# Tap matrices in the array's diagonal quadrants, and another order of the first half blocks, in a convolution followed by a two-layer MLP

## The chip, the cores and the metric

The kernel runs on one core of one Trainium2 chip. The time is device microseconds from launch to end, the median of several runs. A profile covers one execution; its span (first to last instruction) is some 1.7 us less than the time of the same run. Line numbers in profiles are those of the kernel profiled, so the same statement is L341 in one kernel and L356 in another; the tile names say which it is: ph is the first matmul of the MLP, po the second, acc the convolution on TensorE, ptr the transposes, yt the convolution's result, g the activated hidden layer.

## The reference

```python
# x: [8, 4096, 192] f32, weight: [8 heads, 7 taps], w_in: [192, 2048], w_out: [2048, 192]
w = softmax(weight, axis=-1)                      # 7 taps per head, 24 channels share a head
x_pad = concatenate([zeros(B, 6, D), x], axis=1)
out = einsum('hk,bskhg->bshg', w, windows(x_pad))   # causal convolution along the sequence
h = out.reshape(B * S, D) @ w_in
return maximum(0.01 * h, h) @ w_out
```

## The kernel before

Two batch rows are worked on together: partitions 0 to 63 hold 64 channels of one, 64 to 127 the same channels of the other. The sequence is cut into blocks of 512; the first five blocks are handled as ten groups of 256 ("half groups", numbered from 0). Halves 0 to 3 are loaded by plain transfers, cast and transposed on TensorE; later blocks come through transposing transfers. For groups 0 and 1 TensorE does two of the three channel chunks of the convolution, by multiplying with diagonal tap matrices; VectorE does everything else of it, one group ahead of TensorE.

```python
    diag = [const_pool.tile([128, 2, K, 128], BF16, name=f"diag{c}") for c in range(NPEC)]
    def diag_high(c):                     # high bf16 part of the 7 taps: VectorE, 896 elements
        nc.vector.tensor_mul(diag[c][:, 0], ident[:, None, :].to_broadcast([128, K, 128]),
                             wkh[:, c, :, None].to_broadcast([128, K, 128]))
    def diag_low(c, ks):                  # low part: ScalarE, 128 elements a tap
        for k in ks:
            nc.scalar.activation(out=diag[c][:, 1, k, :], in_=ident, func=Copy, scale=wkl[:, c, k : k + 1])
    ...
    load_first(2)
    for job in conv_jobs(groups[0], range(NPEC, NCH)): job()        # third chunk, VectorE
    for c in range(NPEC):                                           # two chunks, TensorE
        pe_jobs, evac_y = pe_conv_jobs(groups[0], c)                # 14 matmuls 128x128 by 128x256
        for job in pe_jobs: job()
        evac_y(act_scale)
        warm(3)
    ...
    for i, grp in enumerate(groups):
        ...
        for j in range(steps):
            for u in range(2 * j, 2 * j + 2):
                mm1(grp, u)               # 12 ph matmuls, then one activation on ScalarE
                ...                       # i == 0: transposes of half 1, TensorE's convolution of group 1
            for _ in range(quota):
                mm2_slot(slot); slot += 1     # po matmuls, two row halves
            for job in ahead[per * j : per * (j + 1)]: job()    # VectorE: convolution of group i+1
            if i == 0 and j == 2:
                for evac_y in evacs: evac_y(nc.vector.tensor_scalar_mul)
                for e in range(2): cast_first(2, e, nc.vector.tensor_copy)
            if i == 1 and j == 2:
                for e in range(2): cast_first(3, e, nc.vector.tensor_copy)
            if i < 2 and j == 3:
                transpose_first(i + 2)
                evac_first(i + 2, nc.vector.tensor_copy, nc.vector.tensor_copy)
```

Of the kernel before, what the change touches and what calls it, by code (L numbers as in the profile page):

```python
# [10 lines left out]
BF16 = mybir.dt.bfloat16  # L11
# [3 lines left out]
def kernel(  # L15
# [8 lines left out]
    nc = tc.nc  # L24

    B, S, D = x.shape
    H, K = weight.shape
# [3 lines left out]
    BASE = HALO - (K - 1)  # L31
# [3 lines left out]
    CH = 64  # L35
    NCH = D // CH
    ST = 512
# [9 lines left out]
    NPEC = 2  # L47

    const_pool = ctx.enter_context(tc.tile_pool(name="const", bufs=1))
# [14 lines left out]
    groups = [(b, h * HT, HT) for b in range(NHALF) for h in range(2)]  # L64
# [3 lines left out]
    x_nat, x_bf, xt = {}, {}, {}  # L68
# [35 lines left out]



    def load_first(q):
        t = stage_pool.tile([128, 2, HS, D], FP32, name="x_nat")
        for e in range(2):
            nc.sync.dma_start(  # L110
                out=t[:, e, :, :],
                in_=x[e, q * HT : (q + 1) * HT, :].rearrange("(c p) d -> p c d", p=128),
            )
        x_nat[q] = t

    def cast_first(q, e, copy):
        if q % 2 == 0 and e == 0:
            x_bf[q // 2] = xb_pool.tile([128, NCH, SUB, 2, CH], BF16, name="x_bf")
        h = q % 2
        copy(  # L120
            out=x_bf[q // 2][:, :, h * HS : (h + 1) * HS, e, :],
            in_=x_nat[q][:, e, :, :].rearrange("p s (c k) -> p c s k", c=NCH),
        )
# [3 lines left out]
    def transpose_first(q):  # L127
        ts = [
            psum_o.tile([128, HS, NCH, CH], BF16, name=f"ptr{i}", tag="po") for i in range(2)
        ]  # L130
        for s in range(HS):
            for c in range(NCH):
                for i in range(2):
                    ps = slice(i * CH, (i + 1) * CH)
                    nc.tensor.transpose(  # L135
                        out=ts[i][:, s, c, :],
                        in_=x_bf[q // 2][ps, c, (q % 2) * HS + s, :, :].rearrange(
                            "p e k -> p (e k)"
                        ),
                        identity=ident[ps, ps],  # L140
                    )
        ptr[q] = ts

    def evac_first(q, *copies):
        dst = xt[0][:, :, HALO + q * HT : HALO + (q + 1) * HT].rearrange(
            "p c (s i k) -> p i s c k", s=HS, i=2
        )
        for i, t in enumerate(ptr.pop(q)):
            copies[i](out=dst[:, i], in_=t)  # L149
# [4 lines left out]
    def conv_jobs(grp, chunks=range(NCH)):  # L154
        blk, t0, T = grp
        rp, st = divmod(blk, NB)
        if blk not in yt:
            yt[blk] = yt_pool.tile([128, NCH, ST], BF16, name="yt")
        y = yt[blk]
        jobs = []  # L160
        for c in chunks:
            for k in range(K):
                a = BASE + k + st * ST + t0
                src = xt[rp][:, c, a : a + T]
                dst = y[:, c, t0 : t0 + T]
                if k == 0:
                    jobs.append(
                        lambda s=src, d=dst, c=c: nc.vector.tensor_scalar_mul(  # L168
                            d, s, wk[:, c, 0:1]
                        )  # L170
                    )
                else:
                    jobs.append(
                        lambda s=src, d=dst, c=c, k=k: nc.vector.scalar_tensor_tensor(  # L174
                            out=d, in0=s, scalar=wk[:, c, k : k + 1], in1=d,
                            op0=mybir.AluOpType.mult, op1=mybir.AluOpType.add,
                        )
                    )
        return jobs

    def pe_conv_jobs(grp, c):


        blk, t0, T = grp
        acc = psum_o.tile([128, ST], FP32, name="acc", tag="po")
        jobs = []
        for p in range(2):
            for k in range(K):
                jobs.append(
                    lambda k=k, p=p: nc.tensor.matmul(  # L190
                        out=acc[:, :T], lhsT=diag[c][:, p, k, :],
                        rhs=xt[0][:, c, BASE + k + blk * ST + t0 : BASE + k + blk * ST + t0 + T],
                        start=(k == 0 and p == 0), stop=(k == K - 1 and p == 1),
                    )
                )
        return jobs, lambda scale: scale(yt[blk][:, c, t0 : t0 + T], acc[:, :T], rsum[:, c, :])  # L196


# [8 lines left out]
    nc.vector.memset(junk, 0.0)  # L207
    ident = const_pool.tile([128, 128], BF16)
    make_identity(nc, ident)

    sel = const_pool.tile([H, NCH, 2, CH], FP32, name="sel")
    nc.gpsimd.memset(sel, 1.0)  # L212
    for sign, off in ((1, 0), (-1, GRP - 1)):
        nc.gpsimd.affine_select(  # L214
            out=sel, in_=sel, compare_op=mybir.AluOpType.is_ge, fill=0.0,
# [4 lines left out]
    w_in = const_pool.tile([128, NCH, F], BF16)  # L220
    for q in range(WQ):
        for e in range(2):
            fs = slice(q * F // WQ, (q + 1) * F // WQ)
            nc.gpsimd.dma_start(  # L224
                out=w_in[e * CH : (e + 1) * CH, :, fs],
                in_=moe_w_in[:, fs].rearrange("(c p) f -> p c f", p=CH),
# [7 lines left out]
    def warm(n):  # L234
# [9 lines left out]
        out=nmax, in_=w9[:, 0:K], axis=mybir.AxisListType.X,  # L244
# [3 lines left out]
        out=w9[:, 0:K], in_=w9[:, 0:K], func=mybir.ActivationFunctionType.Exp,  # L248
# [4 lines left out]
    for c in range(NCH):  # L253
        nc.tensor.matmul(
            out=wps[:, 0, c * (K + 1) : (c + 1) * (K + 1)],
# [12 lines left out]
    nc.vector.tensor_sub(wkl, wraw[:, :, 0:K], wkh)  # L268


    diag = [const_pool.tile([128, 2, K, 128], BF16, name=f"diag{c}") for c in range(NPEC)]

    def diag_high(c):
        nc.vector.tensor_mul(  # L274
            diag[c][:, 0],
            ident[:, None, :].to_broadcast([128, K, 128]),
            wkh[:, c, :, None].to_broadcast([128, K, 128]),
        )

    def diag_low(c, ks):  # L280
        for k in ks:
            nc.scalar.activation(  # L282
                out=diag[c][:, 1, k, :], in_=ident,
                func=mybir.ActivationFunctionType.Copy, scale=wkl[:, c, k : k + 1],
            )

    transpose_first(0)
    warm(3)
    diag_high(0)
    diag_low(0, range(2))  # L290
    evac_first(0, nc.vector.tensor_copy, nc.scalar.copy)
    diag_low(0, range(2, K))
    diag_high(1)
    diag_low(1, range(K))
    rsum = const_pool.tile([128, NCH, 1], FP32)
# [7 lines left out]
            out=out, in_=in_, func=mybir.ActivationFunctionType.Copy, scale=scale  # L303
        )

    load_first(2)
    for job in conv_jobs(groups[0], range(NPEC, NCH)):
        job()
    for c in range(NPEC):
# [99 lines left out]
    for i, grp in enumerate(groups):  # L409
        blk, t0, T = grp  # L410
        steps = T // 64
        if t0 == 0:
            g[blk] = g_pool.tile([128, NFC, 2, ST], BF16, name="g", tag="g")
        quota = (avail - slot) // steps

        if i == 0:
            ahead, pe_ahead = [], []
        else:
            ahead = conv_jobs(groups[i + 1]) if i + 1 < len(groups) else []
        per = -(-len(ahead) // (steps - 1)) if T == ST else -(-len(ahead) // steps)  # L420
        for j in range(steps):
            for u in range(2 * j, 2 * j + 2):
                mm1(grp, u)
                if i == 0 and u == 1:
                    transpose_first(1)
                    evac_first(1, nc.vector.tensor_copy, nc.vector.tensor_copy)
                    ahead = conv_jobs(groups[1], range(NPEC, NCH))
                    evacs = []
                    for c in range(NPEC):
                        pe_jobs, evac_y = pe_conv_jobs(groups[1], c)  # L430
                        pe_ahead += pe_jobs
                        evacs.append(evac_y)
                    per = len(ahead)
                if i == 0 and u in (3, 5):
                    for job in pe_ahead[: 2 * K]:
                        job()
                    pe_ahead = pe_ahead[2 * K :]
            for _ in range(quota):
                mm2_slot(slot)
                slot += 1  # L440
            for job in ahead[per * j : per * (j + 1)]:
                job()
            if i == 0 and j == 2:
                for evac_y in evacs:
                    evac_y(nc.vector.tensor_scalar_mul)
                for e in range(2):
                    cast_first(2, e, nc.vector.tensor_copy)
            if i == 1 and j == 2:
                for e in range(2):
                    cast_first(3, e, nc.vector.tensor_copy)  # L450
            if i < 2 and j == 3:

                transpose_first(i + 2)
                evac_first(i + 2, nc.vector.tensor_copy, nc.vector.tensor_copy)

            last_half = t0 + T == ST
            if j == steps // 4 and last_half:
                load_x(blk + 3)
            if j == steps // 2 and last_half and blk > 0:
                transpose_x(blk + 2)  # L460
        avail += 2 * T // 128 * NFC
# [37 lines left out]
```

## Time and profile before

| | kernel before |
|---|---|
| time, first three runs | 699.71 us (699.24 to 699.77) |
| span of the profiled run | 697.3 us |
| TensorE busy | 689.5 us, 99% |
| VectorE, ScalarE busy | 541.0 us, 512.2 us |
| first ph matmul, first po matmul | 10.88 us, 23.55 us |
| start of group 2 on TensorE | 33.34 us |

In a timeline row the columns are start, length (both us), engine, line, operation, tiles, shapes, count, and in brackets the idle time before it with what ended it. A matmul row's length includes the last matmul's way through the array, so rows overlap by a little. A waits row gives who waited for whom, total us, times, and the longest.

### The profile page before, as it was taken

Reading aid. Unit: us, or ns where it says so; the run is one execution under the profiler, and the core shown is the slowest. Engines: PE = TensorE matmul, PEld = TensorE weight load, DVE = VectorE, ACT = ScalarE, POOL = GpSimd, SP = SyncE. Lnnn points to the kernel's source line nnn. Section 1 sums busy time; section 2 is a strip of 40 time slices with the busy share of each in tenths; the row PEclk is TensorE's granted clock in tenths of the full one; section 3 lists DMA queues with packets and bytes.
Section 4 is the critical chain, followed back from the end, with each engine's and each line's share of the span. In section 5 each row is a group of like instructions: output and inputs, shape, how many; then the busy total and the mean of one; then the engine's idle time right before and its main releaser. Section 6 shows DMA issues by size and latency. Waiting matters only on the chain.

```text
span 697.3 us, 25946 instructions
## 1 busy us (share of the span) xinstructions
PE 689.5 (99%) x11730; PEld 611.6 (88%) x11730; DVE 541.0 (78%) x995; ACT 512.2 (73%) x574; POOL 142.0 (20%) x198
## 2 busy tenths in 40 slices
PE   8999999999999999999999999999999999999997
PEld 6899998678888888888888888888888888888887
DVE  6799999967777787777787777787777787777712
ACT  6778887977777777777777777777777777777770
POOL 6342221420222211222220222220222211000000
PEclk9999999999999999999999999999999999999999
DMA  9986654855556545557543556534555545112112
GB/s 174 134 89 75 83 79 74 90 72 80 74 66 92 82 66 86 67 74 91 80 75 70 78 73 87 86 68 72 78 75 84 86 67 77 54 51 59 47 36 69
DMA packets 184846, 54.37 MB, mean 78 GB/s; under 512 B 148384, under 2 KB 184736, under 8 KB 184736
## 3 DMA queue, kind: packets, MB, share of 16 engines
q0 software_dynamic: 98768, 14.17, 29.4%
q1 hardware_dynamic: 85968, 38.56, 22.6%
q8 instruction: 91, 1.49, 0.9%
q14 instruction: 19, 0.16, 0.1%
HBM read 29.88 MB, written 25.17 MB: 79 GB/s over the span
## 4 chain that ended last, share of the span: by engine, by line
PE 92%; DVE 4%; DMA 3%; ACT 0%; POOL 0%; issue 0%; POOLq 0%; ACTq 0%
PE po L361 47%; PE ph L341 45%; DVE yt L174 3%; DMA w_out<-in_moe_w_out_dram 2%; DMA w_in<-in_moe_w_in_dram 1%; ACT g L348 0%; DVE yt L168 0%; POOL sel L214 0%; DVE xt L149 0%; POOL sel L212 0%; PE ptr L135 0%; DVE o_sb L400 0%; POOL ident masks.py:199 0%; ACT o_sb L400 0%; POOL ident masks.py:197 0%
## 5 line engine op out<-in xcount | busy, mean ns | idle before, releaser
L348 ACT ACTIVATE g<-ph 128x1024 bf16<-128x1024 f32 x512 | 496.2, 1021 | 165.6 <-PE ph L341 165.6
L174 DVE SCALAR_TENSOR_TENSOR yt<-xt,wk,yt 128x512 bf16<-128x512 bf16 (+1 forms) x642 | 439.7, 685 | 17.4
L361 PE MATMUL po<-w_out,g 64*128 64x192 bf16 (+1 forms) x8048 | 397.8, 243 | 0.1
L361 PEld LDWEIGHTS <-g 64*128 64x128 bf16 (+1 forms) x8048 | 372.1, 94 | 28.8 <-issue 0.4
L341 PE MATMUL ph<-yt,w_in 64*128 64x512 bf16 (+1 forms) x3552 | 391.9, 347 | 2.5 <-DVE yt L174 1.4
L341 PEld LDWEIGHTS <-w_in 64*128 64x128 bf16 x3552 | 249.1, 94 | 48.0 <-issue 5.4
L79 POOL DMA_DIRECT2D x_bf<-in_x_dram x180 | 133.6, 772 | 433.0 <-DMA xt<-x_bf 424.9
L400 DVE COPY o_sb<-po 128x192 f32<-128x192 f32 x216 | 77.3, 358 | 127.2 <-PE po L361 124.8
L168 DVE TENSOR_SCALAR yt<-xt,wk 128x512 bf16<-128x512 bf16 (+1 forms) x107 | 36.4, 340 | 0.2
L400 ACT COPY o_sb<-po 128x192 f32<-128x192 f32 x40 | 13.1, 327 | 0.0
L190 PE MATMUL acc<-xt,diag 128*128 128x256 bf16 x56 | 7.4, 288 | 0.0
L190 PEld LDWEIGHTS <-diag 128*128 128x128 bf16 x56 | 5.6, 103 | 1.6 <-issue 0.4
L236 PE MATMUL warm<-zero 128*128 128x256 bf16 x20 | 4.5, 372 | 1.1 <-DVE junk L207 1.1
L224 POOL DMA_DIRECT2D w_in<-in_moe_w_in_dram x8 | 5.1, 643 | 0.0
L282 ACT ACTIVATE diag<-ident,wkl 128x128 bf16<-128x128 bf16 x14 | 4.3, 391 | 0.1
L236 PEld LDWEIGHTS <-zero 128*128 128x128 bf16 x20 | 2.2, 122 | 1.8 <-DVE junk L207 1.1
L120 DVE CAST x_bf<-x_nat 128x384 bf16<-128x384 f32 x7 | 2.7, 416 | 1.4 <-DMA x_nat<-in_x_dram 1.4
L149 DVE COPY xt<-ptr 128x384 bf16<-128x384 bf16 x7 | 2.2, 354 | 1.8 <-PE ptr L135 1.8
L196 DVE TENSOR_SCALAR yt<-acc,rsum 128x256 bf16<-128x256 f32 x2 | 1.0, 483 | 2.6 <-PE acc L190 2.6
L274 DVE TENSOR_TENSOR diag<-ident,wkh 128x896 bf16<-128x896 bf16 x2 | 2.2, 1082 | 0.0
L135 PEld LDWEIGHTS <-x_bf 64*128 64x128 bf16 x48 | 1.2, 101 | 0.9 <-issue 0.8
L135 PE MATMUL ptr<-ident,x_bf 64*128 64x64 bf16 x48 | 1.7, 202 | 0.2 <-ACT o_sb L400 0.2
(27 smaller groups left out, 11.8 us busy)
## 6 DMA issues: line engine op xcount, KB each, us to landing
out_dram<-o_sb SPq DMA_DIRECT2D x128, 192.0 KB, 2.1
x_bf<-in_x_dram POOLq DMA_DIRECT2D x180, 64.0 KB, 3.5
x_nat<-in_x_dram SPq DMA_DIRECT2D x8, 192.0 KB, 5.9
w_in<-in_moe_w_in_dram POOLq DMA_DIRECT2D x8, 192.0 KB, 9.2
xt<-x_bf SPq DMA_TRANSPOSE x90, 2.4
w_out<-in_moe_w_out_dram POOLq DMA_DIRECT2D x1, 768.0 KB, 14.2
w<-in_weight_dram SPq DMA_DIRECT2D x1, 0.2 KB
```

Of the source, the lines that this page charges most:

```text
L79: nc.gpsimd.dma_start(out=t[:, c, :, e, :], in_=src[2 * rp + e, :, :, c * CH : (c + 1) * CH],)
L135: nc.tensor.transpose(out=ts[i][:, s, c, :], in_=x_bf[q // 2][ps, c, (q % 2) * HS + s, :, :].rearrange("p e k -> p (e k)"), identity=ident ...
L168: lambda s=src, d=dst, c=c: nc.vector.tensor_scalar_mul(d, s, wk[:, c, 0:1])
L174: lambda s=src, d=dst, c=c, k=k: nc.vector.scalar_tensor_tensor(out=d, in0=s, scalar=wk[:, c, k : k + 1], in1=d, op0=mybir.AluOpType.mult, ...
L190: lambda k=k, p=p: nc.tensor.matmul(out=acc[:, :T], lhsT=diag[c][:, p, k, :], rhs=xt[0][:, c, BASE + k + blk * ST + t0 : BASE + k + blk * ...
L224: nc.gpsimd.dma_start(out=w_in[e * CH : (e + 1) * CH, :, fs], in_=moe_w_in[:, fs].rearrange("(c p) f -> p c f", p=CH),)
L236: nc.tensor.matmul(out=wa[:, 0, 0:HT], lhsT=zero[:, 0:128], rhs=zero, start=True, stop=True)
L282: nc.scalar.activation(out=diag[c][:, 1, k, :], in_=ident, func=mybir.ActivationFunctionType.Copy, scale=wkl[:, c, k : k + 1],)
L341: nc.tensor.matmul(out=ph[:, e, i * T : (i + 1) * T], lhsT=w_in[ps, c, f * 128 : (f + 1) * 128], rhs=y[ps, c, t0 : t0 + T], start=(c == 0) ...
L348: act = nc.scalar.activation(out=g[blk][:, nf * u : nf * (u + 1), :, t0 : t0 + T], in_=ph.rearrange("p e (i t) -> p i e t", i=nf), func=my ...
L361: ins = nc.tensor.matmul(out=po[m], lhsT=g[b][ps, fc, e, s * 128 : (s + 1) * 128], rhs=w_out[ps, fc, :], start=(rt != 1 and fc == 0), stop ...
L400: copy(out=o_sb[:, n % 2, :], in_=po.pop(n))
```

## The change

Its intent is to shorten the start and to give VectorE less to do there. Each tap matrix is block diagonal with two equal 64 by 64 blocks, so it is stored folded to 64 columns and used in two diagonal quadrants of the array. The load of half 2 waits for a late instruction of ScalarE, to leave the transfers to w_in. The casts of halves 2 and 3 go from VectorE to ScalarE, the transposes are done earlier, and VectorE starts group 2's convolution before it scales the second chunk of group 1. The diff is abridged, with some lines joined.

```diff
-                        out=acc[:, :T], lhsT=diag[c][:, p, k, :], rhs=xt[0][:, c, ...],
+                for e in range(2):
+                    ps = slice(e * CH, (e + 1) * CH)
+                            out=acc[ps, :T], lhsT=diag[c][ps, p, k, :], rhs=xt[0][ps, c, a : a + T],
...
+    nc.vector.tensor_add(ident2, ident[:, 0:CH], ident[:, CH:128])
-    diag = [const_pool.tile([128, 2, K, 128], BF16, name=f"diag{c}") for c in range(NPEC)]
+    diag = [const_pool.tile([128, 2, K, CH], BF16, name=f"diag{c}") for c in range(NPEC)]
...
-    load_first(2)
+    load_first(2, low)          # the first of its two transfers waits for diag_low(0)
...
+                if i == 0 and u == 2:
+                    for e in range(2): cast_first(2, e, nc.scalar.copy)
+                if i == 0 and u == 4:
+                    transpose_first(2); evacs[0](act_scale)
+                if i == 1 and u in (0, 2): cast_first(3, u // 2, nc.scalar.copy)
...
+            if i == 0 and j == 3:
+                evac_first(2, nc.vector.tensor_copy, nc.vector.tensor_copy)
+                early = conv_jobs(groups[2])
+                for job in early[:4]: job()
+                evacs[1](nc.vector.tensor_scalar_mul)
-            if i == 0 and j == 2: ...   # scalings and casts on VectorE, as shown above
-            if i == 1 and j == 2: ...
-            if i < 2 and j == 3: ...
+            if i == 1 and j == 1: transpose_first(3)
+            if i == 1 and j == 3: evac_first(3, nc.vector.tensor_copy, nc.vector.tensor_copy)
```

More of the change, by code (lines that the diff above doesn't have):

```diff
@@ L103, in new_xt, with load_first @@
         nc.vector.memset(xt[rp][:, :, 0:HALO], 0.0)
-    def load_first(q):
+    def load_first(q, after=None):
         t = stage_pool.tile([128, 2, HS, D], FP32, name="x_nat")
         for e in range(2):
-            nc.sync.dma_start(
+            ins = nc.sync.dma_start(
                 out=t[:, e, :, :],
@@ L113, in load_first @@
             )
+            if after is not None and e == 0:
+                tc.add_manual_dep(
+                    ins.ins, after.ins.name,
+                    mybir.DependencyInfo(
+                        mybir.DependencyClass.Sync, mybir.DependencyReason.DATA
+                    ),
+                    reason="leave the DMA engines to w_in",
+                )
         x_nat[q] = t
@@ L188, in pe_conv_jobs @@
             for k in range(K):
-                jobs.append(
-                    lambda k=k, p=p: nc.tensor.matmul(
-                        out=acc[:, :T], lhsT=diag[c][:, p, k, :],
-                        rhs=xt[0][:, c, BASE + k + blk * ST + t0 : BASE + k + blk * ST + t0 + T],
-                        start=(k == 0 and p == 0), stop=(k == K - 1 and p == 1),
+                a = BASE + k + blk * ST + t0
+                for e in range(2):
+                    ps = slice(e * CH, (e + 1) * CH)
+                    jobs.append(
+                        lambda k=k, p=p, a=a, e=e, ps=ps: nc.tensor.matmul(
+                            out=acc[ps, :T], lhsT=diag[c][ps, p, k, :],
+                            rhs=xt[0][ps, c, a : a + T],
+                            start=(k == 0 and p == 0), stop=(k == K - 1 and p == 1),
+                        )
                     )
-                )
         return jobs, lambda scale: scale(yt[blk][:, c, t0 : t0 + T], acc[:, :T], rsum[:, c, :])
@@ L209 @@
     make_identity(nc, ident)
+    ident2 = const_pool.tile([128, CH], BF16)
+    nc.vector.tensor_add(ident2, ident[:, 0:CH], ident[:, CH:128])
     sel = const_pool.tile([H, NCH, 2, CH], FP32, name="sel")
@@ L275, in diag_high @@
             diag[c][:, 0],
-            ident[:, None, :].to_broadcast([128, K, 128]),
-            wkh[:, c, :, None].to_broadcast([128, K, 128]),
+            ident2[:, None, :].to_broadcast([128, K, CH]),
+            wkh[:, c, :, None].to_broadcast([128, K, CH]),
         )
@@ L281, in diag_low @@
         for k in ks:
-            nc.scalar.activation(
-                out=diag[c][:, 1, k, :], in_=ident,
+            act = nc.scalar.activation(
+                out=diag[c][:, 1, k, :], in_=ident2,
                 func=mybir.ActivationFunctionType.Copy, scale=wkl[:, c, k : k + 1],
             )
+        return act
     transpose_first(0)
@@ L291 @@
     evac_first(0, nc.vector.tensor_copy, nc.scalar.copy)
-    diag_low(0, range(2, K))
+    low = diag_low(0, range(2, K))
     diag_high(1)
@@ L417 @@
             ahead, pe_ahead = [], []
+        elif i == 1:
+            ahead = early[4:]
         else:
@@ L433 @@
                     per = len(ahead)
+                if i == 0 and u == 2:
+                    for e in range(2):
+                        cast_first(2, e, nc.scalar.copy)
+                if i == 0 and u == 4:
+                    transpose_first(2)
+                    evacs[0](act_scale)
                 if i == 0 and u in (3, 5):
-                    for job in pe_ahead[: 2 * K]:
+                    for job in pe_ahead[: 4 * K]:
                         job()
-                    pe_ahead = pe_ahead[2 * K :]
+                    pe_ahead = pe_ahead[4 * K :]
+                if i == 1 and u in (0, 2):
+                    cast_first(3, u // 2, nc.scalar.copy)
             for _ in range(quota):
@@ L440 @@
                 slot += 1
+            if i == 0 and j == 3:
+                evac_first(2, nc.vector.tensor_copy, nc.vector.tensor_copy)
+                early = conv_jobs(groups[2])
+                for job in early[:4]:
+                    job()
+                evacs[1](nc.vector.tensor_scalar_mul)
             for job in ahead[per * j : per * (j + 1)]:
                 job()
-            if i == 0 and j == 2:
-                for evac_y in evacs:
-                    evac_y(nc.vector.tensor_scalar_mul)
-                for e in range(2):
-                    cast_first(2, e, nc.vector.tensor_copy)
-            if i == 1 and j == 2:
-                for e in range(2):
-                    cast_first(3, e, nc.vector.tensor_copy)
-            if i < 2 and j == 3:
-                transpose_first(i + 2)
-                evac_first(i + 2, nc.vector.tensor_copy, nc.vector.tensor_copy)
+            if i == 1 and j == 1:
+                transpose_first(3)
+            if i == 1 and j == 3:
+                evac_first(3, nc.vector.tensor_copy, nc.vector.tensor_copy)
             last_half = t0 + T == ST
```

## The prediction

> **What bounds the kernel now.** I read the page's busy shares first, then the list of what TensorE waited for over the whole span, then the timelines of TensorE, VectorE and ScalarE in the first 50 us and around 120 us.
>
> From the page:
>
> ```profile
> PE 689.5 (99%) x11730; PEld 611.6 (88%) x11730; DVE 541.0 (78%) x995; ACT 512.2 (73%) x574; POOL 142.0 (20%) x198
> PE 92%; DVE 4%; DMA 3%; ACT 0%; POOL 0%; issue 0%; POOLq 0%; ACTq 0%
> ```
>
> TensorE is the bound: 689.5 of 697.3 us, and 92% of the chain that ended last. The 4% on VectorE and 3% on DMA in that chain lie at the start. So the change can win only what TensorE idles, or does besides its matmuls proper. The waits of TensorE over the whole span:
>
> ```profile
> PE ph L341 <- DVE yt L174: 1.4, 2, 0.9
> PE warm L236 <- DVE junk L207: 1.1, 1, 1.1
> PE ph L341 <- ACT g L348: 0.6, 2, 0.3
> PE ph L341 <- DMA w_in<-in_moe_w_in_dram: 0.4, 1, 0.4
> PE ptr L135 <- ACT o_sb L400: 0.2, 1, 0.2
> ```
>
> Columns: total us, times, longest. Without the fixed 1.1 us before the first warm-up matmul that is 2.6 us, all the idle time there is to win. Where it lies, from the timeline of TensorE alone:
>
> ```profile
> 13.68 1.48 PE L341 MATMUL ph<-yt,w_in 64*128 64x256 bf16 x23 [0.38 <-DMA w_in<-in_moe_w_in_dram]
> 21.73 1.75 PE L341 MATMUL ph<-yt,w_in 64*128 64x256 bf16 x24 [0.29 <-ACT g L348]
> 23.55 1.31 PE L361 MATMUL po<-w_out,g 64*128 64x192 bf16 x14
> ...
> 119.66 1.04 PE L341 MATMUL ph<-yt,w_in 64*128 64x512 bf16 x8 [0.93 <-DVE yt L174]
> ```
>
> and from the timeline of all engines at 33 to 45 us:
>
> ```profile
> 33.18 0.33 PE L135 MATMUL ptr<-ident,x_bf 64*128 64x64 bf16 x11 [0.24 <-ACT o_sb L400]
> 44.70 1.27 PE L341 MATMUL ph<-yt,w_in 64*128 64x256 bf16 x20 [0.44 <-DVE yt L174]
> ```
>
> The reader is to see two kinds of wait. At 13.7 us TensorE waits for the weights w_in, and the 23.55 us start of the second matmul is the moment w_out lands (issued at 9.33 us, 14.18 us in the chain, so 23.50). These are transfers. At 44.7 and 119.7 us it waits for VectorE's convolution: one half group of convolution costs VectorE 3 x 3.32 = 9.97 us (the starts 47.88, 51.20, 54.52 of successive chunks), TensorE takes 4 steps of 2.63 = 10.52 us for it, so VectorE gains only 0.55 us a half group. It runs without a gap from 44.6 to beyond 119.5 us; the first group of full blocks (three chunks of 4.98 us) then comes 0.93 us late. Any head start that VectorE gets before 45 us is kept until 119 us.
>
> **What the Trainium skill says.** "TensorEngine Tiling (Array Packing)", under Key Properties and Restrictions: tiles run independently, a change of tiling mode drains the array, and column tiling switches Fast Weight Load off. The trace agrees on the drain: the weight queue shows 0.20 to 0.21 us of "issue" idle at each switch between the convolution and w_in. It has no 64x64 tile, so the other two are untested here. "TensorE: Matmul & The Clock Gate", LDWEIGHTS: a load costs columns / 1.2 ns, so 64 columns would be about 53 ns (an estimate from that page); matmuls of 256 columns in alternating row halves come every 1.31/24 = 54.6 ns in the trace, so such loads would just fit. The same page, Part 3 (what overlaps): matmuls start in strict program order, so one blocked matmul blocks TensorE; the trace agrees at 33.18 us, where a transpose held up everything behind it. "DMA: Bandwidth & Descriptors", Arbitration: the engines take turns between queues. The trace agrees: the load of half 2 issued at 4.85 us, behind and beside others, took 8.4 us to land, against 2.5 us for the first.
>
> **The change part by part.**
>
> *Half-width tap matrices.* VectorE's two products shrink from 896 to 448 elements: 1.08 us each, about 0.61 if some 0.15 us is fixed; 0.47 saved on each. The first saving ends in a wait for the transposes (VectorE's copy out starts at 5.87 us anyway), so 0.47 us reaches the first convolution, which ends at 10.78 instead of 11.25. ScalarE's 14 low parts shrink from 128 to 64 elements; 1021 ns for 1024 elements and 327 for 192 give 0.83 ns an element, so 53 ns less each, 0.64 us over the twelve. The first ph matmuls and their activation thus move from 11.96 to about 11.5 us. But the next pair needs the second quarter of w_in, complete at 13.66 us: TensorE waits longer there instead. TensorE's own convolution goes from 14 matmuls to 28 in two diagonal quadrants; if pairs run together, 14 x 109 = 1.53 us as now. I allow 0.1 us for slower loads, twice, on the path.
>
> *Load of half 2 held back* until ScalarE's low part, about 7.5 us instead of 4.85. In the kernel before, it stood behind halves 0 and 1 until 8.65 us, so only about 1 us of sharing with w_in is removed; w_in's second quarter may come 0.3 us earlier, and half 2 about 0.5 us later (its second piece landed at about 15.8 us, so 16.3). w_out must still follow all of w_in with the same bytes beside it, so I leave it at 23.5 us.
>
> *Casts on ScalarE.* Two casts (0.51 us each, the row of the one ScalarE did at 4.31 us) and one scaling (0.46) join group 0's activations. Followed in order: activation 2 ends at 15.1, the second cast waits for the load, ends at 16.8, activation 3 at 17.8; matmul ph 5 waits for it (0.3 us); transposes of half 2 now stand before it (0.35 us, moved, not added). The last two activations end near 22.2 and 23.2 instead of 21.6 and 22.6, and two ph matmuls wait on them. The first po matmul starts near 23.95 instead of 23.55: **+0.4 us**.
>
> *VectorE order.* Casts of halves 2 and 3 leave it (2 x 0.75 us), and half 2 is copied out at about 17.5 us rather than 21.5, so four operations of group 2's convolution fill the 2.58 us in which VectorE waited for acc. Group 2's convolution: 17 operations are left at 20.9 us, 3 x 0.515 + 2 x 3.41 = 8.4 us, so done at 29.3 instead of 33.0. Group 3's starts at 29.9 instead of 34.2. VectorE gains about 4 us, more than 0.44 + 0.93, and its inputs are there (the transposing load that feeds the first full block lands near 98.8 us; VectorE would want it near 100). Both waits go: **-1.37 us**. The 0.24 us wait of the last transposes for a PSUM slot goes too, as they move two steps earlier: **-0.24 us**.
>
> *A new wait.* In the built program the third po accumulator takes the PSUM slot of half 3's transposes, and waits for VectorE's copy of it, which stands behind all of group 2's convolution: free at about 29.6 us. TensorE comes there at 28.78 + 0.35 (moved transposes) + 0.4 = 29.5. **+0.1 us**, and up to 1 if VectorE is late.
>
> Sum: -1.37 - 0.24 + 0.4 + 0.1 + 0.2 (quadrants) - 0.2 (part of the earlier weights) = **-1.1 us**: 699.71 - 1.1 = **698.6 us**.
>
> **The rivals.** (1) The quadrants don't overlap, because they write one PSUM bank, or the slower loads set the pace. For: nothing in the trace has this form. Against: row halves pair well (54.6 ns). Unpaired, each of the two convolutions in group 0 takes 3.06 us instead of 1.53: +3 us there, and the new wait grows no further, as both engines shift; about 701. (2) The new wait is the cost of the head start: if half 2 lands at 18 us rather than 16.3, ScalarE, in order, stalls, all of group 0 slips by up to 1.5 us, and VectorE's copy with it; about 700. For: half 2's loads took 8.4 to 10 us. (3) The transfers were the whole bound of the start and the delay gives w_in more than I think, so that group 0 runs 0.5 to 1 us earlier and w_out follows: 697.5. Against: w_out's 14.18 us are full of traffic either way. (4) The head start is lost before 119 us, to late transposing loads or buffers, and only 0.44 + 0.24 is won: 699.5.
>
> **Range and chances.** The ends come from rival 3 with all gains (697.2) and from rival 2 or half of rival 1 (700.3). Two per cent is 14 us; everything before the first activation (11.96 us) is shorter than that, and TensorE's steady work isn't touched. So within 2%: 0.98.
>
> **What would show each step.** VectorE's product at half width near 0.61 us; the first activation near 11.5 us; 28 quadrant matmuls in about 1.5 to 1.7 us (3 would be rival 1); first po matmul at 23.5 to 24.0; a TensorE wait on VectorE's copy of half 3 before the third accumulator of at most 0.4 us; no waits on the convolution near 44 and 119 us. The prediction is wrong if group 0's matmuls slip by over 1 us, if the wait at 119 us stays, or if w_out lands earlier by a microsecond.

## The result, and the profile after

The changed kernel took 699.04 us (698.09 to 700.15, six runs), the kernel before 700.07 us over its six runs. The ratio is 0.9985 (95% interval 0.9972 to 0.9998). Ratios here are the mean time of one kernel's runs over that of the other's of the same rounds, so not quite the ratio of the medians. Run again beside other kernels, it took 698.35 against 699.49 us, ratio 0.9982 (0.9969 to 0.9996). So it is about 0.15% faster, the same by the measure of 2%.

The span went from 697.3 to 696.4 us. TensorE's waits over the whole span, changed kernel:

```profile
PE ph L356 <- ACT g L363: 1.3, 3, 0.6
PE warm L250 <- DVE junk L218: 1.1, 1, 1.1
PE ptr L143 <- ACT x_bf L128: 0.3, 1, 0.3
```

The waits for the convolution (1.4 us), for w_in (0.4 us) and of the last transposes (0.2 us) are gone. The waits for ScalarE's activation doubled, from 0.6 to 1.3 us, and a wait for a cast is new. Where these lie, in the timeline of TensorE of the changed kernel:

```profile
9.02 1.72 PE L201 MATMUL acc<-xt,diag 64*64 64x256 bf16 x28
10.67 0.50 PE L250 MATMUL warm<-zero 128*128 128x256 bf16 x3
11.11 1.58 PE L356 MATMUL ph<-yt,w_in 64*128 64x256 bf16 x24
...
17.57 0.35 PE L143 MATMUL ptr<-ident,x_bf 64*128 64x64 bf16 x12 [0.27 <-ACT x_bf L128]
18.48 0.83 PE L356 MATMUL ph<-yt,w_in 64*128 64x256 bf16 x12 [0.57 <-ACT g L363]
19.25 1.72 PE L201 MATMUL acc<-xt,diag 64*64 64x256 bf16 x28
...
22.85 1.75 PE L356 MATMUL ph<-yt,w_in 64*128 64x256 bf16 x24 [0.46 <-ACT g L363]
24.41 1.32 PE L376 MATMUL po<-w_out,g 64*128 64x192 bf16 x14
```

and in the timeline of ScalarE what held them up:

```profile
17.00 0.51 ACT L128 CAST x_bf<-x_nat 128x384 bf16<-128x384 f32 x1 [1.57 <-DMA x_nat<-in_x_dram]
17.42 1.93 ACT L363 ACTIVATE g<-ph 128x1024 bf16<-128x1024 f32 x2
```

ScalarE ran its operations in program order here. It stood idle for 1.57 us until the second transfer of half 2 had landed at 16.98 us, and the activations behind the cast came that much later. The chain that ended last agrees. For the changed kernel, over the first 60 us, it runs through that transfer (start, length):

```profile
7.83 0.15 SPq L110
7.98 0.04 issue
8.02 8.96 DMA x_nat<-in_x_dram
16.98 0.02 issue
17.00 0.51 ACT x_bf L128
```

In the kernel before, the chain ran through the transfers of w_in and w_out to 23.5 us:

```profile
9.33 14.18 DMA w_out<-in_moe_w_out_dram
```

The other side of the ledger is VectorE. It starts group 3's convolution at 34.20 us in the kernel before,

```profile
34.20 0.29 DVE L168 TENSOR_SCALAR yt<-xt,wk 128x256 bf16<-128x256 bf16 x1
```

and 4.06 us earlier in the changed kernel:

```profile
30.14 0.29 DVE L176 TENSOR_SCALAR yt<-xt,wk 128x256 bf16<-128x256 bf16 x1
```

The ledger on TensorE: group 2 starts at 33.85 us instead of 33.34, **0.51 us later**. From there to the end of the span it takes 696.4 - 33.85 = 662.55 us instead of 697.3 - 33.34 = 663.96, **1.41 us less**, which is, within the rounding of the spans, the two waits for the convolution (0.44 + 0.93 = 1.37). The net is 0.9 us.

### The profile page after: what moved, and what is told of

Its sections match the earlier page's. It is cut to its first block, busy times and chain, and to the rows that moved or that the text cites. A ratio compares the mean times of both kernels' runs of the same rounds, so it can differ in the third digit from the quotient of the medians.

```text
span 696.4 us, 26058 instructions
## 1 busy us (share of the span) xinstructions
PE 689.5 (99%) x11786; PEld 612.7 (88%) x11786; DVE 538.2 (77%) x991; ACT 513.3 (74%) x579; POOL 142.1 (20%) x198
## 4 chain that ended last, share of the span: by engine, by line
PE 97%; DMA 1%; ACT 1%; POOL 0%; issue 0%; DVE 0%; SPq 0%; POOLq 0%; ACTq 0%
PE po L376 49%; PE ph L356 47%; DMA x_nat<-in_x_dram 1%; ACT g L363 1%; PE acc L201 0%; PE wps L268 0%; ACT diag L296 0%; POOL sel L228 0%; PE warm L250 0%; PE ptr L143 0%; ACT x_bf L128 0%; ACT xt L157 0%; POOL sel L226 0%; DVE o_sb L415 0%; POOL ident masks.py:199 0%
## 5 line engine op out<-in xcount | busy, mean ns | idle before, releaser
L415 ACT COPY o_sb<-po 128x192 f32<-128x192 f32 x40 | 13.1, 327 | 0.0
L201 PE MATMUL acc<-xt,diag 64*64 64x256 bf16 x112 | 7.3, 280 | 0.0
L201 PEld LDWEIGHTS <-diag 64*64 64x64 bf16 x112 | 6.0, 111 | 1.2 <-issue 0.6
L128 ACT CAST x_bf<-x_nat 128x384 bf16<-128x384 f32 x5 | 2.5, 507 | 3.6 <-DMA x_nat<-in_x_dram 3.6
L296 ACT ACTIVATE diag<-ident,wkl 128x64 bf16<-128x64 bf16 x14 | 3.6, 339 | 0.0
L128 DVE CAST x_bf<-x_nat 128x384 bf16<-128x384 f32 x3 | 1.2, 439 | 1.4 <-DMA x_nat<-in_x_dram 1.4
L317 ACT ACTIVATE yt<-acc,rsum 128x256 bf16<-128x256 f32 x3 | 1.4, 470 | 1.2 <-PE acc L201 1.2
L268 PEld LDWEIGHTS wps<-w,sel 8*128 8x128 f32 x6 | 1.4, 322 | 0.7 <-POOL sel L228 0.7
```

What stands on the lines that cost most here:

```text
L128: copy(out=x_bf[q // 2][:, :, h * HS : (h + 1) * HS, e, :], in_=x_nat[q][:, e, :, :].rearrange("p s (c k) -> p c s k", c=NCH),)
L201: lambda k=k, p=p, a=a, e=e, ps=ps: nc.tensor.matmul(out=acc[ps, :T], lhsT=diag[c][ps, p, k, :], rhs=xt[0][ps, c, a : a + T], start=(k == ...
L296: act = nc.scalar.activation(out=diag[c][:, 1, k, :], in_=ident2, func=mybir.ActivationFunctionType.Copy, scale=wkl[:, c, k : k + 1],)
L415: copy(out=o_sb[:, n % 2, :], in_=po.pop(n))
```

## The experiments

Twelve kernels, two of them repeats, were run in three batches, each batch on one chip beside the kernel before. The interval of each ratio is about 0.13% to either side, 0.9 us, so the time alone rarely tells two variants apart; the traces do. I compare two stretches: from the first ph matmul to the start of group 2 ("front"), and from there to the end ("rest"). The last four columns are those of the one profiled run of each; the kernel before has only one trace, so its front has no repeat.

| kernel | time, kernel before (us) | ratio | first ph | group 2 | front | rest |
|---|---|---|---|---|---|---|
| before | 699.71 | | 10.88 | 33.34 | 22.46 | 663.96 |
| changed | 699.04, 700.07 | 0.9985 | 11.11 | 33.85 | 22.74 | 662.55 |
| changed, again | 698.35, 699.49 | 0.9982 | 11.69 | 34.17 | 22.48 | 662.53 |
| no hold | 698.27, 699.62 | 0.9979 | 11.21 | 32.86 | 21.65 | 662.54 |
| no hold, again | 698.20, 699.35 | 0.9978 | 12.03 | 34.05 | 22.02 | 662.55 |
| cast on VectorE | 698.01, 699.62 | 0.9977 | 11.09 | 33.53 | 22.44 | 662.27 |
| no hold, cast on VectorE | 698.50, 699.49 | 0.9981 | 12.49 | 34.52 | 22.03 | 662.28 |
| taps only | 699.52, 699.49 | 1.0001 | 12.10 | 33.85 | 21.75 | 664.55 |
| order only | 698.08, 699.49 | 0.9976 | 11.57 | 33.31 | 21.74 | 662.59 |
| full taps (its slowest run) | 698.84, 699.62 | 0.9990 | 11.16 | 37.82 | 26.66 | 662.58 |
| no warm-up | 699.28, 699.62 | 0.9994 | 11.13 | 34.62 | 23.49 | 662.58 |
| no hold, no warm-up | 698.18, 699.35 | 0.9980 | 11.42 | 33.50 | 22.08 | 662.50 |
| late VectorE, 5 | 699.05, 699.35 | 0.9994 | 12.57 | 34.43 | 21.86 | 662.47 |
| late VectorE, 10 | 701.67, 699.35 | 1.0029 | 11.54 | 35.03 | 23.49 | 665.17 |

The first ph matmul differs between runs of the same kernel by 0.6 to 0.8 us; the reason is shown under "no warm-up". A later start leaves less to wait for transfers, so a front is compared best at a like start.

### The theory and its rivals

Theory A: the gain is VectorE's head start, which takes away the two waits; the half-width taps are worth nothing; and the held-back load costs about 1 us in group 0, as ScalarE waits for it. Rivals: the taps or the hold carry part of the gain; or the two extra casts of work, not the wait, are the loss.

### e1_no_hold: the load not held back

```diff
-    load_first(2, low)
+    load_first(2)
```

> The changed kernel, with the load of half 2 not held back. Theory A (the held load is now on the path: its second piece lands at 16.98 us instead of about 15.9, and ScalarE, in order, makes TensorE wait 0.27 and 0.57 us): the piece lands near 16 us, both waits fall to about 0, the wait for w_in near 13.7 us comes back with 0.3 to 0.4 us, the first po matmul moves from 24.41 to about 23.9 us, group 2 starts at about 33.4 instead of 33.85 us, span 0.3 to 0.5 us shorter than the changed kernel. Rival B (holding it back pays, as w_in would otherwise be later by as much): group 2 starts at 33.85 us or later.

Measured: 698.27 us, ratio 0.9979, span 695.4 us. Timelines of this kernel, ScalarE:

```profile
15.14 0.92 ACT L128 CAST x_bf<-x_nat 128x384 bf16<-128x384 f32 x2
15.96 1.03 ACT L363 ACTIVATE g<-ph 128x1024 bf16<-128x1024 f32 x1
```

and TensorE:

```profile
13.25 1.74 PE L356 MATMUL ph<-yt,w_in 64*128 64x256 bf16 x24 [0.28 <-ACT g L363]
...
17.42 0.82 PE L356 MATMUL ph<-yt,w_in 64*128 64x256 bf16 x12
```

Both casts run without a wait, and the ph matmul that stood at 18.48 us comes at 17.42 with no wait named. Group 2 starts at 32.86, 0.99 us sooner than in the changed kernel. The expected return of the w_in wait did not happen: at 13.25 us TensorE waits for its accumulator (0.28 us, as in the changed kernel), not for w_in. Half 2's second transfer had landed at 15.17 us, sooner than the 16 us expected, and the gain is larger than the 0.5 us expected. So against this run the hold bought nothing and cost some 1 us. By the time alone, 0.9979 against 0.9985 isn't separated.

### e3_cast_dve: the hold kept, the second cast back on VectorE

```diff
-                        cast_first(2, e, nc.scalar.copy)
+                        cast_first(2, e, nc.vector.tensor_copy if e else nc.scalar.copy)
```

> The changed kernel with the second cast of half 2 back on VectorE. Theory A (ScalarE's wait for the load is what delays its activations): ScalarE's third activation pair no longer waits for the load, the 0.57 us wait of the ph matmul at 18.48 us goes, group 0 ends 0.6 us sooner, the first po matmul at 23.6 to 23.9 us instead of 24.41; part of it is given back at the third po accumulator, which waits for VectorE's copy of half 3 (up to 0.4 us); group 2 starts 0.2 to 0.6 us sooner. Rival B (two extra casts of work on ScalarE, not the wait for the load, are the loss): at most the 0.5 us of one cast, and the wait at 18.48 us stays above 0.3 us.

Measured: 698.01 us, ratio 0.9977, span 695.8. TensorE's timeline of this kernel:

```profile
13.70 1.48 PE L356 MATMUL ph<-yt,w_in 64*128 64x256 bf16 x23 [0.31 <-DMA w_in<-in_moe_w_in_dram]
...
17.75 0.83 PE L356 MATMUL ph<-yt,w_in 64*128 64x256 bf16 x12
...
24.16 1.31 PE L376 MATMUL po<-w_out,g 64*128 64x192 bf16 x14 [0.31 <-DMA w_out<-in_moe_w_out_dram]
```

The wait at 18.48 us is gone, as theory A said: it was ScalarE's standing still for the load, and moving one cast of 0.5 us won 0.7 us there. In this run, with the hold, TensorE did wait 0.31 us for w_in, so the hold doesn't make sure that w_in is there; and the first po matmul at 24.16 missed the 23.6 to 23.9 expected, because w_out itself landed late. Group 2 starts 0.32 us sooner than in the changed kernel.

### e9_no_hold_dve: both

> The changed kernel without the hold and with the second cast of half 2 on VectorE. Theory A (both remove the same wait, so they do not add): group 2 starts within 0.3 us of the 32.86 us of the run without the hold, and the third po accumulator waits 0.2 to 0.4 us for VectorE's copy of half 3, as VectorE has 0.4 us more to do. Rival B (they add): 0.4 us or more below the run without the hold.

Measured: 698.50 us, ratio 0.9981, span 696.8; front 34.52 - 12.49 = 22.03 us. Its first ph matmul came late, so the absolute start of group 2 can't be compared; by the front, the two do not add. TensorE goes on from the ph matmuls before the third po accumulator 0.20 us late (30.57 us instead of 29.06 + 1.31), in the direction of theory A.

### e5_taps_only and e6_order_only: the two halves of the change alone

The first is the kernel before with the quadrants and folded matrices. The second is the changed kernel with full-width matrices and no hold:

```diff
-    diag = [const_pool.tile([128, 2, K, CH], BF16, ...   # and pe_conv_jobs, ident2: as before the change
+    diag = [const_pool.tile([128, 2, K, 128], BF16, ...
-    load_first(2, low)
+    load_first(2)
```

> The kernel before with the half-width taps in the diagonal quadrants alone. Theory A (they are worth nothing in time: the 0.47 us on VectorE meets the 0.4 us of mode changes around the warm-up matmuls, then the wait for w_in): the waits of 0.44 us near 44.7 and 0.93 us near 119.7 us stay within 0.2 us, span within 0.3 us of the kernel before. Rival B (the quadrants pay): span 0.5 us shorter or more.

> The changed kernel with full-width taps and without holding the load back, so that only the casts on ScalarE and VectorE's order are changed against the kernel before. Theory A (these carry the whole gain): waits near 44.7 and 119.7 us gone, no wait of the transposes of half 3 on ScalarE, group 2 starts at 32.8 to 33.2 us, span about 1.5 us under the kernel before, as in the run without the hold. Rival B (half-width taps or the hold are needed for it): span less than 1 us under.

Measured: the taps alone 699.52 us, ratio 1.0001 (0.9989 to 1.0014); the order alone 698.08 us, ratio 0.9976 (0.9963 to 0.9988). TensorE's waits, taps only:

```profile
PE ph L348 <- DVE yt L174: 1.9, 2, 1.2
PE ptr L135 <- ACT o_sb L407: 0.2, 1, 0.2
```

and order only:

```profile
PE warm L244 <- DVE junk L215: 1.1, 1, 1.1
PE ph L350 <- ACT g L357: 0.7, 2, 0.5
```

With the taps alone both waits on the convolution stay. At 0.70 and 1.24 us they exceed the 0.44 and 0.93 us of the kernel before by more than the 0.2 us I allowed. The traces show where: two of the products that begin a chunk of group 3's convolution took 0.58 and 0.63 us there and 0.30 and 0.66 us in the kernel before, 0.25 us more together, while most take 0.28 us; why they vary is not shown. With the order alone they are gone and the rest is 662.59 us, that of the changed kernel. Group 2 began at 33.31 us, 0.11 above the range given, with a first ph matmul at 11.57 us. So the order of VectorE, with the casts on ScalarE, carries the whole gain, and neither the half-width taps nor the hold is needed. How much of VectorE's head start comes from the moved casts, from the earlier transposes and from the earlier start of group 2's convolution was not separated; with one cast of half 2 back on VectorE (e3, e9) the rest stayed at 662.3 us.

### e4_full_taps: the changed kernel with full-width matrices

> The changed kernel with full-width tap matrices as in the kernel before. Theory A (the half-width taps are worth nothing in time here): VectorE's two products back at 1.08 us, its first convolution ends at 11.25 instead of 10.78 us, the convolutions of group 0 take the same 1.5 to 1.7 us on TensorE, group 2 starts within 0.15 us of 33.85 us, and the waits at 44 and 119 us stay away; span within 0.2 us of the changed kernel. Rival B (the taps carry part of the gain): span 0.4 to 0.6 us longer.

Measured: 698.84 us median, ratio 0.9990 (0.9976 to 1.0003), which would agree with theory A, but not tightly. The profiled run was the slowest of the five, 702.10 us against 698.35 to 699.96, and can't test group 2's start. What it can test agrees: no wait on the convolution came back, and the rest is 662.6 us, so the whole of its delay lies in the front. It shows the hold at its worst, in TensorE's timeline:

```profile
20.01 0.35 PE L143 MATMUL ptr<-ident,x_bf 64*128 64x64 bf16 x12 [2.35 <-ACT x_bf L128]
20.93 0.83 PE L350 MATMUL ph<-yt,w_in 64*128 64x256 bf16 x12 [0.57 <-ACT g L357]
21.69 2.92 PE L198 MATMUL acc<-xt,diag 128*128 128x256 bf16 x14
```

Half 2 landed at about 19.4 us; TensorE idled 2.35 us, and then ran at a granted clock of 0.50 from 22 to 24 us and 0.65 to 26, so the convolution took 2.92 instead of 1.71 us. Here a late load cost twice.

### e2_no_warm and e10_no_hold_no_warm: without the warm-up matmuls between the convolutions

```diff
         evac_y(act_scale)
-        warm(3)
```

> The changed kernel without the two times three warm-up matmuls after the two convolutions of half 0, which now need a change of tiling mode on either side. Theory A (those matmuls and mode changes ate the 0.47 us that the half-width taps won, but behind them the held load sets the pace): first ph matmul at about 10.65 instead of 11.11 us, first activation at 11.5 instead of 12.07, but the ph matmul after the transposes of half 2 still at 18.4 to 18.5 us, span unchanged within 0.1 us. Rival B (the start of the ph matmuls sets the pace): everything up to 45 us moves by 0.4 to 0.5 us and the span is as much shorter.

> The changed kernel without the hold and without the six warm-up matmuls after the convolutions of half 0. Theory A (with the load off the path the start of the ph matmuls counts): first ph matmul 0.4 us sooner than with them at the same moment of TensorE's change to its full rate, which differs from run to run between 7.6 and 10.4 us; group 2 starts 21.4 to 21.8 us after the first ph matmul; in the mean of the runs 0 to 0.4 us under the run without the hold. Rival B (the warm-up matmuls keep TensorE's rate up): the full rate comes later in the trace and the mean is 0.5 us longer.

Measured: 699.28 us, ratio 0.9994, and 698.18 us, ratio 0.9980; the runs without the hold but with the warm-up matmuls gave 0.9979 and 0.9978. The first is inconclusive: its first ph matmul came at 11.13 us and not at 10.65, because TensorE ran at half its rate until about 9.3 us. In the second, the first ph matmul at 11.42 us soon waited 0.35 us for ScalarE, and the front was 33.50 - 11.42 = 22.08 us against the 21.4 to 21.8 expected. No gain shows in the mean of either. A loss of 0.5 us does not show in the second; by the ratios the first is 0.6 to 0.8 us longer than the changed kernel, which is within the noise.

What they did show is why runs differ. The warm-up matmuls are a clock one can read. In the changed kernel:

```profile
5.78 0.82 PE L250 MATMUL warm<-zero 128*128 128x256 bf16 x3
6.52 2.13 PE L201 MATMUL acc<-xt,diag 64*64 64x256 bf16 x28
8.58 0.50 PE L250 MATMUL warm<-zero 128*128 128x256 bf16 x3
```

and in the kernel with the cast on VectorE and no hold (e9):

```profile
6.52 3.19 PE L201 MATMUL acc<-xt,diag 64*64 64x256 bf16 x28
9.64 0.82 PE L250 MATMUL warm<-zero 128*128 128x256 bf16 x3
10.40 1.72 PE L201 MATMUL acc<-xt,diag 64*64 64x256 bf16 x28
```

Three warm-up matmuls take 0.82 us at half rate and 0.50 at full. Full rate came at about 7.4 us in the first run (not 7.6, as the expectation above has it) and about 10.4 in the second, with the same instructions on TensorE up to there; the profile page's granted clock, 1.00 throughout, does not show it. The first ph matmul moved from 11.11 to 12.49 us with it.

### e7_late5 and e8_late10: taking VectorE's head start away

```diff
                 evac_first(3, nc.vector.tensor_copy, nc.vector.tensor_copy)
+                for _ in range(5):        # 10 in the second
+                    nc.vector.scalar_tensor_tensor(out=scrap, in0=xt[0][:, 0, HALO : HALO + HT],
+                        scalar=wk[:, 0, 1:2], in1=zero, op0=mult, op1=add)
```

> The changed kernel with five more products of 256 elements on VectorE (about 0.515 us each, 2.6 us in all, results unused) behind the copy of half 3. Theory A (VectorE's head start is only a reserve; in the changed kernel it is done with the first full block 3.1 us before TensorE needs it, 115.3 against 118.4 us): no wait on the convolution near 44 or 119 us, the time is that of the changed kernel within 0.2 us. Rival B (an earlier VectorE is worth its whole amount): 2 us longer or more.

> As before with ten such products, 5.15 us. Theory A (the reserve is 4.3 us at the wait near 44 us and 3.1 us at the one near 119 us): a wait of 0.8 to 0.9 us near 45 us, one of 1.1 to 1.3 us near 119 us, together 2.0 us, and the stretch from the start of group 2 to the end 2.0 us longer than in the changed kernel (662.55 us). Rival B (the waits went for another reason): none of these waits.

Measured: 699.05 us, ratio 0.9994, and 701.67 us, ratio 1.0029 (1.0015 to 1.0042). With five, TensorE waits for the convolution nowhere and the rest is 662.47 us, the changed kernel's. By the ratios its time is 0.6 to 0.8 us above the changed kernel's, where I had expected 0.2 at most; that is within the noise, and the trace, of its fastest run, shows no cause for it. With ten, TensorE's waits:

```profile
PE ph L357 <- DVE yt L182: 2.3, 2, 1.3
```

They are 1.06 us before the matmul at 47.01 us and 1.28 us before that at 122.32 us, against 0.8 to 0.9 and 1.1 to 1.3 expected. The rest is 665.17 us, 2.6 us longer than the changed kernel's; 2.0 was expected, and 0.3 of it is not in these two waits. So 2.6 us of the head start may be lost for nothing, while a loss of 5.15 us cost 2.3 us in waits: the head start is a reserve, and its size is about what I read off the timelines. With the order-only kernel this shows the cause of the gain in both directions.

### after_again and e11_no_hold_again: repeats

> The changed kernel once more, in the rounds of the others. If its loss in group 0 is systematic, the second piece of half 2 again lands near 17 us, ScalarE's wait for it and the ph matmul's wait of about 0.57 us come back, and the span is about 1 us under that of the kernel before; if it was that run's DMA, the waits are gone and the span is 695.5.

> The changed kernel without the hold, again. If the hold costs what the first trace said, group 2 starts 21.6 to 21.9 us after the first ph matmul (22.74 and 22.48 us in the two traces of the changed kernel), ScalarE does not wait for the load of half 2, and the ratio to the kernel before is again 0.998. If the first run was luck of its transfers, 22.4 us or more.

Measured: the changed kernel again 698.35 us, ratio 0.9982, span 696.7, which is 0.6 us under the kernel before and not 1; ScalarE waited 1.31 us for half 2's second transfer, and TensorE 0.57 us behind it, as the first time. That loss is systematic. Without the hold again 698.20 us, ratio 0.9978, span 696.6; ScalarE did not wait. Its front, 22.02 us, is 0.1 above the range, owing to a wait that the prediction had named:

```profile
30.11 1.50 PE L376 MATMUL po<-w_out,g 64*128 64x192 bf16 x32 [0.36 <-DVE xt L157]
```

The third po accumulator waited for VectorE's copy of half 3. What the hold does can be read from all the traces by when the transfers landed. With it, the second transfer of half 2 landed at 16.98 to 19.42 us (seven traces), without it at 15.17 to 16.29 us (seven, the kernel before with 15.30 among them). The second quarter of w_in, for which the hold makes room, did land earlier with it, at 13.1 instead of 13.6 us in the mean. In the five traces with the hold in which ScalarE casts both transfers and TensorE kept its full rate (the changed kernel twice, e2, e7, e8), the first po matmul came 7.43 to 7.44 us after half 2's landing, whenever the ph matmuls had begun. Without the hold (e1, e6, e11) it came 12.1 to 12.3 us after the first ph matmul; with it (the changed kernel twice, e7, e8) 12.4 to 13.7 us. So the hold cost some 0.2 to 1.5 us, the least where TensorE began latest (e7).

Is there a version that beats both? The kernels without the hold had ratios 0.9976 to 0.9981 (five kernels), the changed kernel 0.9982 and 0.9985, and with the hold but one cast back on VectorE (e3) it was 0.9977. The traces favour the former, but the intervals overlap, so I don't claim it from the times.

## Why the prediction was right

698.6 us from 699.71 is a ratio of 0.9984; measured were 0.9985 and 0.9982. That the two agree to 0.1 us is in part luck: the interval of a ratio is 0.9 us to either side, and misses cancel. In the traces, the first po matmul was to move by +0.4 us (casts, quadrants, earlier weights) and moved by +0.86; the stretch from there to group 2 was to change by -0.14 us (transposes, new wait) and changed by -0.35; the rest was to change by -1.37 us and changed by -1.41. The sum is -0.9 us, where -1.1 was predicted. By its steps:

- *VectorE order, -1.37 us*: right. Both waits went, the rest of the span fell by 1.41 us, group 3's convolution began at 30.14 us (predicted 29.9, from 34.2). The order alone did it (e6), and taking the head start away brought the waits back (e8).
- *Transposes of half 3, -0.24 us*: right in kind, too small. That wait is in no trace with the new order. From the first of these transposes to the next ph matmul it was 0.59 us before (32.75 to 33.34) and 0.18 us after (28.34 to 28.52), 0.41 us less.
- *Casts on ScalarE, +0.4 us*: the mechanism was right, the size off. The first po matmul came at 24.41 us instead of the predicted 23.95, so the loss was 0.86 us. The mis-sized term is the landing of half 2: 16.98 us, not 16.3. I had read its landing in the kernel before as 15.8 us, and the trace has 15.30 (issued at 5.26 us, 10.0 us to landing), so the hold moved it by 1.7 us and not by 0.5. The held load started later and then took 9 us beside w_in and w_out; the repeat had a like wait. Why standing behind the earlier halves did not make up for the later issue, as I had reckoned, is not shown. Part of my second rival was thus true.
- *The new wait at the third po accumulator, +0.1 us*: right, 0.07 us in the changed kernel (1.39 instead of 1.32 us in the chain), and up to 0.36 us in others.
- *Half-width taps*: VectorE's product took 0.62 us (0.61 predicted) and its convolution ended at 10.8 us (10.78), but the step to an activation at 11.5 us failed: it came at 12.07. The last input was not VectorE's chunk but TensorE's second, which was scaled from 10.78 us on. The warm-up matmuls, of 128 rows, now stand between convolutions in quadrants, and at each such change of mode the weight queue was idle for 0.20 or 0.21 us (lines below the list). TensorE itself loses less: across a change its matmuls start 0.20 us apart instead of 0.11 us, so one costs some 0.09 us, and the quadrants bring four more of them before the first ph matmul. The taps alone gave a ratio of 1.0001. The sum didn't suffer, as I had let w_in swallow the gain anyway.
- *Quadrants, +0.2 us; rival 1*: rejected. 28 matmuls in quadrants took 1.72 us, 14 full ones 1.71, and the two of a pair start within 5 ns of each other, so the pairs run together at full speed.
- *Hold, -0.2 us*: not borne out. The step from an earlier w_in to less waiting failed. w_in's second quarter did land earlier (12.26 instead of 13.63 us), and w_in was no reason to wait in the changed kernel (0.38 us before). But it wasn't without the hold either, as TensorE waited 0.28 us for its accumulator there anyway, and with the hold it was in e3 (0.31 us) and e4 (0.20 us). The hold's cost was some 0.2 to 1.5 us.

The weight queue at two changes of mode, in the changed kernel:

```profile
8.58 0.22 PEld L250 LDWEIGHTS <-zero 128*128 128x128 bf16 x3 [0.20 <-issue]
9.01 1.46 PEld L201 LDWEIGHTS <-diag 64*64 64x64 bf16 x28 [0.21 <-issue]
```

What I had not foreseen at all is the instant of full rate on TensorE, which moves the first ph matmul by up to 1.5 us between runs (11.09 us in e3, 12.57 in e7), more than the whole effect of this change. Without the hold the first po matmul moves with it; with the hold it followed half 2's landing instead.

## What to carry to other kernels

An engine that is not the bound but feeds it is best judged by its reserve at each place where the bound engine waits: a head start pays until the reserve is positive everywhere, and nothing beyond. Before putting a cast that depends on a transfer on an engine that works in order, look at what stands behind it: here 0.5 us of work was harmless, while 1.6 us of waiting in front of it held up the bound engine. And an operation made cheaper in one place can cost a change of tiling mode in another, so count the neighbours too.

## What the Trainium skill lacked or had wrong

- "TensorEngine Tiling (Array Packing)", Restrictions and Gotchas, says that different row tiles cannot access the same PSUM bank at the same time. As it stands this is too wide. Here two diagonal 64x64 quadrants, which differ in rows and in columns, accumulate in one bank on different partitions, with correct results and no loss: 28 matmuls in 1.72 us against 1.71 us for 14 full ones.
- The same page, Key Properties: a mode change drains the array, without a figure. The traces show 0.20 to 0.21 us of idle in the weight queue at each, and at full rate 0.20 us from one matmul's start to the next across it, instead of 0.11.
- The same page, Restrictions: column tiling turns Fast Weight Load off, without saying what that costs. No cost shows here: 28 loads of 64x64 went by in 1.46 us, 52 ns apart, hidden under pairs of matmuls 109 ns apart, if only just.
- "TensorE: Matmul & The Clock Gate", Part 1, gives about 4 us of sustained activity until full rate, within 0.5 us from run to run, though it also calls the warm-up run-variable. Here the first matmul ran at 1.13 us with short gaps after it, and full rate came at about 7.4 us in one run and 10.4 in another, a spread of 3 us. The profile's granted clock read 1.00 meanwhile.
- The same page has the clock fall after one idle window of some 3.4 us. In e4 TensorE did nothing but 0.35 us of transposes from 17.65 to 20.93 us, 3.3 us, which is near that figure. What the run adds is that the clock fell only at about 22.0 us, after another 1 us of matmuls at full rate.
